# Attention and MoE on one core: DMA transposes replaced by PE transposes, weights cast by DMA, x in a ring

## The chip, the cores and the metric

The kernel runs on one core of one Trainium2 chip. The metric is the device time of one execution in microseconds (us); the median of several runs is quoted. "Span" is the time from the first to the last instruction in the profiled execution; it is about 2 us shorter than the time. The names of engines: PE is the matmul engine, ACT ScalarE, DVE VectorE, Pool GpSimd, SP the engine that here only issues DMAs.

## The reference, cut to what matters

Attention over 8 batches, 8 heads, 576 tokens, head size 64, with a causal window of 128 and an ALiBi bias; its output, as x of 4608 tokens by 512, goes through a two-layer network:

```python
scores = (1/8) * q @ k.T + slopes[h] * -(i - j)     # kept where 0 <= i - j < 128
x = softmax(scores) @ v                             # -> [8 * 576, 512]
h = x @ w_in                                        # [4608, 2048]    "moe1"
out = (h * cos(h)) @ w_out                          # [4608, 512]     "moe2"
```

Inputs and output are float32; the kernel computes in bf16 with float32 sums.

## The kernel before

Tokens go through moe1 and moe2 in nine chunks of 512; attention goes by batches of 576. After a start (loads, masks, attention of batch 0), seven stages alternate: moe1 of chunk c, 64 dense matmuls, then attention of batch c + 1, whose short matmuls are filled up with the 64 moe2 matmuls of chunk c. A tail finishes the last two chunks.

Attention needs q and k with the head dimension on the partitions, and moe1 needs x so. For batches 1 to 7 all three are transposed by the DMA engines, issued from SP.

```python
def dma_transposes(b):                     # q and k of batch b, two DMAs each
    for which in ("q", "k"):
        fns = [lambda e: e.dma_start_transpose(<blocks 0 to 3 of tr[which][b % 2]>, nat[which] ...),
               lambda e: e.dma_start_transpose(<block 4>, ...)]
        op("sp", fns, ...)
...
def x_dma(b, pr):                          # x of batch b, one pair of heads, 512 tokens
    ...
    fns.append(lambda e, o=o, i=i: e.dma_start_transpose(o, i))
    op("sp", fns, r=[("xnat", b % 2, pr, 0), ("xnat", b % 2, pr, 1)],
       w=[("xT", b, pr)] + (stages if t0 + 512 > XA else []), dma=f"x{pr}{b % 2}")
```

`op` records what an operation reads (`r`) and writes (`w`) and puts the waits in. Tokens beyond 2560 (`XA`) have their x in a buffer that is the weights' staging buffer under another name, so `w` names all its parts (`stages`). The loop (cut) runs over nine units of attention a batch, one of tails and eight of a pair of heads and half of the tokens. `scores` is the product of q and k (PE), `exps` the exponential (ACT), `mask` the multiplication by the mask (DVE), `pv` the product with v (PE), `norm` the division by the sum of a row (DVE); `take(n)` issues the next n fill matmuls, those of moe2:

```python
take(lead)                                 # lead = 8 moe2 matmuls
for j in range(2): scores(us[j]); exps(us[j])
for j in range(n):                         # n = 9
    take(per)                              # per = 4 moe2 matmuls, ahead of the scores
    mask(us[j])
    if j + 2 < n: scores(us[j + 2]); exps(us[j + 2])
    if j >= 1: norm(us[j - 1]); after_norm(us[j - 1])    # issues x_dma
    pv(us[j])
    if mid is not None and j == n // 2: mid()
...
def mid(c=c):                              # in the middle of attention of batch c + 1
    if c + 2 < B: dma_transposes(c + 2); load_v(c + 2)
    if c + 3 < B: load_nat("q", q, c + 3); load_nat("k", k, c + 3)
```

The weights come as float32 through a staging buffer by SP and are cast to bf16 by DVE.

The softmax here doesn't subtract the row's maximum and nothing guards it: scores larger than these inputs give would overflow.

## Time and profile before

446.1 us (445.0 to 448.9, 3 runs); span 444.3 us.

| part | us of the span | what shows |
|---|---|---|
| start | 0 to 48.6 | attention of batch 0 waits for q's copies, which stand behind weight casts on DVE, and then for v |
| seven stages | 48.6 to 385.5: 46.0, 47.3, 45.4, 57.1, 53.4, 45.2, 42.6 | PE waits for DMA before moe1 |
| tail | 385.5 to 444.3 | PE dense |

From the page of the kernel before: PE's busy tenths and the granted PE clock in 40 slices of 11 us, and the chain of work that ended last.

```profile
PE   0057798849794979697840997619885988899996
PEclk9999998969897898989895798958998898999999
...
PE 53%; DMA 19%; DVE 12%; SPq 6%; ACT 5%; issue 2%; POOL 2%; DVEq 0%; ACTq 0%; POOLq 0%
```

PE is often below nine tenths, and the clock falls with it. SPq, SP's issue queue, has 6% of the chain. The table of waits, PE's lines: what PE waited for, us in total, times, the longest.

```profile
PE ps L610 <- DMA wstage<-xnat: 35.4, 4, 16.7
PE ps L610 <- DMA xTa<-xnat: 16.9, 3, 6.4
PE ps L487 <- DVE xnat L512: 14.3, 7, 2.1
...
PE ps L487 <- DVE p L453: 8.6, 10, 1.1
```

L610 is moe1, L487 the product with v (PV). So PE waits 52.3 us for x's transposes ahead of moe1, and 22.9 us inside attention.

The table of stretches (window; its length; busy us of PE, weight loads, DVE, ACT, Pool with counts; PE clock; DMA share; GB/s) gives the start of moe1 of stage 1, that moe1, its attention, and a moe1 with a wait of only 1.3 us before it:

```profile
94.50:98.00 3.50, 3.48 (x9) 1.30 (x10) 0.69 (x1) 0.69 (x1) 3.05 (x4) 0.50 2.14 198
94.50:110.70 16.20, 16.13 (x64) 6.94 (x66) 9.72 (x15) 10.31 (x15) 3.05 (x4) 0.86 1.06 81
110.70:135.40 24.70, 20.74 (x189) 9.57 (x190) 13.83 (x33) 11.39 (x12) 4.74 (x6) 0.93 0.64 95
385.50:399.50 14.00, 13.91 (x64) 6.39 (x66) 9.70 (x15) 10.30 (x15) 0.00 (x0) 1.00 0.08 30
```

Behind the wait the clock is 0.50 for 3.5 us, and moe1 takes 16.2 us instead of 14.0.

### The profile page before, as it was taken

What the parts mean: (1) busy time and instruction counts of PE and PEld (TensorE: products, weight loads), DVE (VectorE), ACT (ScalarE), POOL (GpSimd) and SP (SyncE); (2) the same over time, 40 slices, a digit from 0 to 9 for tenths busy, and PEclk for the clock granted to TensorE, in tenths of its full rate; (3) what the DMA queues carried; (4) which work ended last, traced back from release to release, by engine and by line L of the source; (5) the groups of instructions that cost most, each with busy time, mean ns of one, the idle gap of its engine ahead of it and who ended that gap; (6) DMA issues with size and microseconds to landing.
All of it is one profiled execution on the core that took longest, in us unless ns stands there. A gap on an engine that the chain in (4) does not pass through costs nothing.

```text
span 444.3 us, 5753 instructions
## 1 busy us (share of the span) xinstructions
PE 329.3 (74%) x2231; PEld 152.1 (34%) x2268; DVE 228.9 (52%) x444; ACT 190.8 (43%) x245; POOL 97.8 (22%) x123
## 2 busy tenths in 40 slices
PE   0057798849794979697840997619885988899996
PEld 0044343314341434243320443304342433444442
DVE  2737795617560666266620456406572556474531
ACT  3044584317540664077410573206750673374320
POOL 8801047370037001710064000820000000000000
PEclk9999998969897898989895798958998898999999
DMA  9999599994199906990499004990064002300111
GB/s 221 266 270 130 194 156 133 173 190 27 31 137 188 60 26 116 189 86 26 81 145 130 36 1 95 163 157 0 8 122 127 0 2 65 84 0 25 43 51 72
DMA packets 166363, 44.76 MB, mean 101 GB/s; under 512 B 154560, under 2 KB 159680, under 8 KB 166336
## 3 DMA queue, kind: packets, MB, share of 16 engines
q0 software_dynamic: 104224, 14.16, 53.3%
q1 hardware_dynamic: 62112, 30.22, 27.8%
q8 instruction: 18, 0.29, 0.3%
q14 instruction: 9, 0.07, 0.0%
HBM read 36.70 MB, written 9.44 MB: 104 GB/s over the span
## 4 chain that ended last, share of the span: by engine, by line
PE 53%; DMA 19%; DVE 12%; SPq 6%; ACT 5%; issue 2%; POOL 2%; DVEq 0%; ACTq 0%; POOLq 0%
PE ps L610 29%; PE ps L632 17%; DMA wstage<-xnat 11%; DMA vp<-in_v_dram 5%; DMA xTa<-xnat 4%; DVE ob L637 2%; DVE p L453 2%; SPq L552 2%; PE ps L487 2%; DVE gT L618 2%; PE ps L415 2%; ACT L430 2%; SPq L258 2%; SPq L261 2%; DVE xnat L512 2%
## 5 line engine op out<-in xcount | busy, mean ns | idle before, releaser
L615 ACT ACTIVATE cos<-ps,halfpi 128x512 f32<-128x512 f32 x144 | 98.8, 687 | 144.4 <-PE ps L610 143.9
L618 DVE TENSOR_TENSOR gT<-ps,cos 128x512 bf16<-128x512 f32 x144 | 98.8, 690 | 108.6 <-ACT cos L615 108.6
L632 PE MATMUL ps<-w_outb,gT 128*128 128x512 bf16 x552 | 140.4, 391 | 1.9 <-issue 0.9
L610 PE MATMUL ps<-xTa,w_inb 128*128 128x512 bf16 x312 | 78.9, 415 | 35.4 <-DMA xTa<-xnat 16.9
L439 ACT ACTIVATE p<-ps 128x768 bf16<-128x768 f32 x64 | 58.0, 917 | 67.2 <-PE ps L415 62.9
L610 PE MATMUL ps<-wstage,w_inb 128*128 128x512 bf16 x251 | 63.2, 404 | 19.1 <-DMA wstage<-xnat 18.7
L632 PEld LDWEIGHTS ps<-w_outb,gT 128*128 128x128 bf16 x576 | 52.5, 100 | 54.7 <-issue 4.9
L240 POOL DMA_DIRECT2D qnat<-in_q_dram x35 | 29.8, 875 | 167.6 <-DMA qt<-qnat 167.6
L610 PEld LDWEIGHTS ps<-xTa,w_inb 128*128 128x128 bf16 x320 | 33.4, 106 | 80.6 <-issue 48.9
L637 DVE COPY ob<-ps 128x512 f32<-128x512 f32 x36 | 24.9, 691 | 56.6 <-PE ps L632 56.6
L610 PEld LDWEIGHTS ps<-wstage,w_inb 128*128 128x128 bf16 x256 | 26.1, 103 | 53.8 <-issue 27.3
L487 PE MATMUL ps<-vp,p 128*128 128x65 bf16 x256 | 25.3, 207 | 22.9 <-DVE xnat L512 14.3
L453 DVE TENSOR_TENSOR p<-p,emask 128x768 bf16<-128x768 bf16 x64 | 39.5, 616 | 0.4
L249 POOL DMA_DIRECT2D vp<-in_v_dram x40 | 34.0, 900 | 11.7 <-issue 11.7
L240 POOL DMA_DIRECT2D knat<-in_k_dram x35 | 30.1, 883 | 13.5 <-DMA kt<-knat 13.2
L487 PEld LDWEIGHTS ps<-vp,p 128*128 128x128 bf16 x256 | 18.3, 105 | 34.1 <-DVE xnat L512 15.9
L522 DVE TENSOR_TENSOR xnat<-ps,rec 128x256 bf16<-128x256 f32 x64 | 27.2, 424 | 2.2
L415 PE MATMUL ps<-qt,kt 64*128 64x128 bf16 (+1 forms) x320 | 26.7, 269 | 1.1 <-ACT ptail L430 0.8
L490 PE MATMUL ps<-vp,p 128*128 128x65 bf16 x192 | 22.6, 206 | 0.0
L415 PEld LDWEIGHTS ps<-qt,kt 64*128 64x128 bf16 x320 | 11.4, 100 | 27.0 <-issue 14.3
L367 PE MATMUL ps<-ident,gT 128*64 128x128 bf16 x72 | 4.5, 314 | 21.6 <-DVE qt L380 11.0
L521 DVE RECIPROCAL rec<-ps 128x4 f32<-128x4 f32 x64 | 11.4, 177 | 13.8 <-PE ps L490 12.8
(47 smaller groups left out, 127.0 us busy)
## 6 DMA issues: line engine op xcount, KB each, us to landing
out_dram<-ob SPq DMA_DIRECT2D x36, 256.0 KB, 2.3
wstage<-in_moe_w_in_dram SPq DMA_DIRECT2D x8, 512.0 KB, 12.5
vp<-in_v_dram POOLq DMA_DIRECT2D x32, 128.0 KB, 6.7
wstage<-in_moe_w_out_dram SPq DMA_DIRECT2D x8, 512.0 KB, 9.3
qnat<-in_q_dram POOLq DMA_DIRECT2D x28, 128.0 KB, 6.5
knat<-in_k_dram POOLq DMA_DIRECT2D x28, 128.0 KB, 6.1
gT<-in_q_dram POOLq DMA_DIRECT2D x2, 288.0 KB, 7.4
gT<-in_k_dram POOLq DMA_DIRECT2D x2, 288.0 KB, 10.6
```

The source lines that it names most:

```text
L240: fns.append(lambda e, t=t, rows=rows: e.dma_start(nat[which][0:rows, t, :, :], src[b, :, 128 * t:128 * t + rows, :].rearrange("h p d -> p ...
L249: fns.append(lambda e, t=t, rows=rows: e.dma_start(vp[b % 2][0:rows, t, :, 0:64], v[b, :, 128 * t:128 * t + rows, :].rearrange("h p d -> p ...
L415: ins = e.matmul(ps[:, banks[x], c0:c1], keys_ap(b, x, pr, kc), query_ap(b, x, pr, qb, nb), start=True, stop=True)
L439: op("act", lambda e: e.activation(P[i][:, :, lo:512], ps[:, 2 * slot:2 * slot + 2, lo:512], ACTF.Exp, scale=0.125), w=[("B", 2 * slot), ( ...
L453: op("dve", lambda e: e.tensor_tensor(P[i][:, :, lo:512], P[i][:, :, lo:512], EM[:, 2 * pr:2 * pr + 2, lo:512], ALU.mult), r=[("P", i), "E ...
L487: ins = e.matmul(o, P[i][:, x, d0:d0 + 128], V[:, kc, h, 0:65], start=True, stop=not two)
L522: op("dve", lambda e: e.tensor_tensor(o, U[:, :, :, 0:64], rv[:, :, :, None].broadcast_to([128, 2, 2, 64]), ALU.mult), r=[("rec", n % 2)], ...
L610: ins = e.matmul(ps[:, bank, :], w_in[:, kc, 128 * fc:128 * fc + 128], rhs, start=(kc == 0), stop=(kc == NPAIR - 1))
L615: op("act", lambda e: e.activation(cosb[ci][:, :], ps[:, bank, :], ACTF.Sin, bias=halfpi[:, 0:1]), r=["halfpi"], w=[("B", bank), ("cos", ci)])
L618: op("dve", lambda e: e.tensor_tensor(gT[gi][:, fc, :], ps[:, bank, :], cosb[ci][:, :], ALU.mult), r=[("cos", ci)], w=[("B", bank), ("g", ...
L632: op("pe", lambda e: e.matmul(ps[:, bank, :], gT[gi][:, fc, 128 * t:128 * t + 128], w_out[:, fc, :], start=(fc == 0), stop=(fc == NFC - 1) ...
L637: op("dve", lambda e: e.tensor_copy(ob[oi][:, :], ps[:, bank, :]), w=[("B", bank), ("ob", oi)])
```

## The change

Its intent: no DMA transposes at all. q and k come in long rows (2304 bytes each) and are transposed on PE, in moe1, for every batch; x is transposed on PE unit by unit and copied out by ACT into a ring of three chunks; the weights are cast on the way in by DMAs from Pool, so that staging buffer and DVE casts go; v of batch 0 comes ahead of the weights. The masks have the band in the exponent, so no DVE multiply. The fill is split, two moe2 matmuls ahead of the scores and three ahead of PV. The diff, cut to its core:

```diff
-        stage = sb("wstage", [128, NST, 1024], F32)
-        xTa = sb("xTa", [128, NPAIR, XA])
-        xTb = stage[...]...
+        XR = 3 * CH
+        xT = sb("xT", [128, NPAIR, XR])
...
+        def load_w_in(u):
+            op("pool", lambda e: e.dma_start(
+                w_in[:, :, 512 * u:512 * u + 512],
+                moe_w_in[:, 512 * u:512 * u + 512].rearrange("(k p) c -> p k c", p=128)),
+               w=[("wi", u)], dma=f"wi{u}")
...
+        def x_back(b, u, n, eng):
+            bank = ubanks(u, n)[0]
+            dst = ps[:, bank, :].bitcast(BF16)[:, 768:1024]
...                    two PE transposes of 128 x 128, then the copy on ACT
+            for j in range(n + 2):
+                take(part[0] if j < n else last)
+                if 2 <= j:
+                    x_back(b, us[j - 2], j - 2, "act")
+                if j + 2 < n:
+                    scores(b, us[j + 2], j + 2)
+                    exps(b, us[j + 2], j + 2)
+                if j < n:
+                    take(part[1])
+                    pv(b, us[j], j)
+                if j + 1 < n:
+                    mask(b, us[j + 1])
+                if j < n:
+                    norm(b, us[j], j)
...
+                steps = iter(qk_transposes([6, 7], ["dve", "act"]))
                 for fc in range(NFC):
                     moe1(c, fc)
-                    if c == 0 and fc % 2 == 1:
-                        cast_w(8 + fc // 2, "dve")
+                    if fc % 2 == 1:
+                        next(steps)()
...
-                attention(c + 1, moe2_steps(c), 8, 4, mid=mid)
+                attention(c + 1, moe2_steps(c), (8, (2, 3), 3))
```

## The prediction

> **What bounds the kernel now.** The matmul engine (PE) is busy 329 of 444 us, yet the chain of waits gives it only 53%, and DMA 19%. The time is a start (to 48.5 us), seven stages (to 385.5 us: moe1 of a chunk, then attention of the next batch filled with moe2) and a tail (58.8 us).
>
> - Start: attention of batch 0 waits for v until 32.0 us (timeline; 22.4 us of v's DMA in the chain), because the weights share the DMA engines.
> - Stages take 46, 47, 46, 57, 53, 45, 42 us. By the table of waits, PE before moe1 waits 16.9 us for x's DMA transposes into xTa and 35.4 us into the weight staging: 52 us. Behind each gap the clock comes back at 0.50 (94.5 to 98 us), and moe1 takes 16.2 us against 13.9 where there was no gap (385.5 to 399.5): 2.3 us six times. The Trainium skill, "TensorE: Matmul & The Clock Gate", part 1, says that an idle window halves the PE clock; the trace agrees.
> - Tail: PE dense at clock 0.99 to 1.00; untouched.
>
> **The change, costed.** Removed: 52 us of waits, about 14 us of cold restarts, 16 weight casts on DVE (12 us). Added per stage:
> - q/k transposes: batch 0 did 36 in 2.13 us, so 72 take 4.3 us of PE; eight evacuations, four on DVE (0.82 us), four on ACT (0.74 us). In moe1 DVE and ACT then need 14.3 and 15.2 us of 18: hidden; PE's 4.3 us are not.
> - x transposes: 20, about 1.2 us of PE, and nine ACT copies of about 0.4 us, hidden unless a bank waits for them.
> - Attention with moe2 has about 19.5 us of warm PE work and took 20 to 25; five fill matmuls a unit in place of four should close the 2.1 and 1.0 us gaps before PV. I estimate 22.5 us with x.
>
> Stage: 18.2 + 22.5 = about 41 us; seven are 287, against 337.
>
> Start: DMAs by GpSimd alone moved 155 GB/s written, 310 read (30 to 41 us). q, k and v are 3.5 MB and land near 15 us; attention of batch 0, bound by latency at about 1.5 us a unit, ends near 31; w_in is there by 28, q and k of batch 1 by 35, w_out by 48, v by 51 us (15.5 MB): just in time. Moe1 starts near 32 us, 16 earlier.
>
> Sum: 32 + 287 + 59 = 378 us of span, 380 with the 2 us between span and time. With a little for stalls: **383 us, eight times in ten 366 to 405.** Faster by over 2%: 0.95; within 2%: 0.03; slower: 0.02.
>
> **What would show each step.** No DMA wait of PE before moe1 after the first stage; moe1 matmuls at about 216 ns from the first; moe1 with transposes 18 us; stages of 40 to 42 us; first moe1 at 30 to 35 us; about 16 ACT table loads; mean clock over 0.95; PE busy over 85%.
>
> **What would make it wrong.**
> 1. The clock. The same page, part 4, says that transposes don't count as PE activity. 1.0 us of them after each 1.7 us of matmuls may drop the clock: moe1 phases of 21 us or more, 20 us in all. Batch 0's transposes ran at clock 1.00, but with no matmuls around them.
> 2. Weights cast by DMA slower than 300 GB/s read, or w_out and v of batch 1 late: stage 0 stalls by 5 to 10 us.
> 3. ACT in strict order: an x copy queued behind an exp holds a bank, and PV waits, about 0.5 us a unit: 30 us in all.
> 4. The start's latency chain per unit no shorter than before: 5 us.

## More of the kernel before

In the start, DVE's timeline and PE's waits show two things behind each other:

```profile
15.10 0.85 DVE L298 CAST w_inb<-wstage 128x1024 bf16<-128x1024 f32 x1 [2.58 <-DMA wstage<-in_moe_w_in_dram]
21.43 0.82 DVE L380 COPY qt<-ps 128x640 bf16<-128x640 bf16 x1
PE ps L473 <- DMA vp<-in_v_dram: 2.7, 1, 2.7
```

Four weight casts, each waiting for its weights, and then the masks stand on DVE ahead of q's first copy, at 21.4 us although q had landed at 10.1; v landed last, at 31.9, but cost PE only 2.7 us more.

One view I did not look at closely before predicting is SP's timeline (start, us, engine line, operation), here of stage 0:

```profile
75.23 1.19 SPq L552 DMA_TRANSPOSE xTa<-xnat  x1
76.47 3.14 SPq L258 DMA_TRANSPOSE qt<-qnat  x1
79.65 1.26 SPq L261 DMA_TRANSPOSE qt<-qnat  x1
80.95 2.14 SPq L258 DMA_TRANSPOSE kt<-knat  x1
83.13 1.53 SPq L261 DMA_TRANSPOSE kt<-knat  x1
84.71 0.58 SPq L640 DMA_DIRECT2D out_dram<-ob  x1
85.33 4.77 SPq L552 DMA_TRANSPOSE xTa<-xnat  x3
```

One pair of heads of x is issued at 75.2; then SP spends 8.2 us on issuing q and k of the next batch, which nobody needs before the next attention, a whole moe1 later; the other three pairs of x, which moe1 needs at once, go out from 85.3 on. Their norms had ended at 80.4, 82.6 and 84.7 us; they landed at 92.2, 93.0 and 94.3.

## The result, and the profile after

366.0 us (365.6 to 367.2, 4 runs) against 446.3 us (4 runs). The outputs are right. A ratio here is the mean time of one kernel's runs over that of the other's of the same rounds, so not quite the ratio of the medians; it is 0.82, with a 95% interval of 0.816 to 0.824. The direction was right and well within what was called likely, but the time is at the very edge of the range (366 to 405), 17 us below the 383 that was named. The lines of the page that answer to those of before:

```profile
PE   0688999999999999999999999999999999999996
PEclk9955999999999999999999999999999999999999
...
PE 79%; ACT 10%; DVE 6%; DMA 2%; issue 1%; POOL 1%; ACTq 0%; DVEq 0%; POOLq 0%
```

From slice 5 on PE is busy nine tenths or more at full clock; DMA has 2% of the chain instead of 19%. PE's lines in the table of waits (L290: q/k transposes, L342: scores, L414: PV, L505: moe1), the longest and those for moe1 and PV:

```profile
PE ps L290 <- DMA qrows<-in_q_dram: 8.8, 1, 8.8
PE ps L342 <- ACT ptail L357: 4.4, 7, 0.6
...
PE ps L414 <- DVE rec L443: 0.8, 5, 0.2
PE ps L414 <- ACT xT L487: 0.7, 2, 0.5
...
PE ps L505 <- ACT xT L487: 0.2, 1, 0.2
```

The 52.3 us ahead of moe1 are 0.2 us; the 22.9 us ahead of PV are under 3 (1.8 on L414). The stretches: moe1 of stage 1 with its 72 transposes, its attention, and the moe1 of the tail without transposes.

```profile
71.93:89.84 17.91, 17.91 (x139) 7.94 (x137) 13.78 (x20) 13.43 (x21) 1.32 (x3) 1.00 0.20 37
89.84:111.07 21.23, 20.44 (x212) 10.36 (x211) 13.33 (x32) 14.20 (x26) 5.37 (x7) 1.00 0.80 104
306.73:320.55 13.82, 13.82 (x66) 6.27 (x64) 10.41 (x16) 10.97 (x16) 0.00 (x0) 1.00 0.05 20
```

| part | before | predicted | after |
|---|---|---|---|
| first moe1 starts at | 48.6 | 32 | 30.6 |
| seven stages together | 337.0 | 287 | 276.0 (41.1, then six times 39.1) |
| tail | 58.8 | 59 | 58.7 |

### The profile page after: what moved, and what is told of

Its sections match the earlier page's. It is cut to its first block, busy times and chain, and to the rows that moved or that the text cites. A ratio compares the mean times of both kernels' runs of the same rounds, so it can differ in the third digit from the quotient of the medians.

```text
span 365.3 us, 7057 instructions
## 1 busy us (share of the span) xinstructions
PE 341.4 (93%) x2912; PEld 164.6 (45%) x2912; DVE 233.1 (64%) x446; ACT 234.5 (64%) x352; POOL 61.3 (17%) x89
## 4 chain that ended last, share of the span: by engine, by line
PE 79%; ACT 10%; DVE 6%; DMA 2%; issue 1%; POOL 1%; ACTq 0%; DVEq 0%; POOLq 0%
PE ps L505 33%; PE ps L528 30%; PE ps L290 5%; PE ps L342 5%; ACT cos L511 3%; ACT L357 2%; DMA krows<-in_k_dram 2%; PE ps L414 2%; ACT ptail L357 2%; PE ps L473 2%; PE ps L417 1%; ACT kt L303 1%; DVE kt L306 1%; DVE ob L533 1%; DVE gT L514 1%; DVE p L380 1%
## 5 line engine op out<-in xcount | busy, mean ns | idle before, releaser
L528 PE MATMUL ps<-w_outb,gT 128*128 128x512 bf16 x576 | 151.4, 380 | 0.0
L505 PE MATMUL ps<-xT,w_inb 128*128 128x512 bf16 x576 | 138.5, 384 | 0.2 <-ACT xT L487 0.2
L505 PEld LDWEIGHTS ps<-xT,w_inb 128*128 128x128 bf16 x576 | 52.6, 98 | 62.2 <-issue 2.4
L366 ACT ACTIVATE p<-ps 128x768 bf16<-128x768 f32 (+1 forms) x64 | 57.6, 915 | 6.2 <-PE ps L342 6.2
L487 ACT ACTIVATE xT<-ps 128x256 bf16<-128x256 bf16 (+3 forms) x80 | 28.9, 363 | 48.5 <-PE ps L473 42.8
L380 DVE TENSOR_TENSOR p<-p,emask 128x768 bf16<-128x768 bf16 (+1 forms) x64 | 39.5, 616 | 1.1 <-ACT p L366 0.9
L210 POOL DMA_DIRECT2D qrows<-in_q_dram x16 | 10.1, 640 | 172.4 <-PE ps L290 171.6
L342 PE MATMUL ps<-qt,kt 64*128 64x128 bf16 (+1 forms) x320 | 24.6, 248 | 5.4 <-ACT ptail L357 4.4
L414 PEld LDWEIGHTS ps<-vp,p 128*128 128x128 bf16 x256 | 18.3, 100 | 17.4 <-ACT xT L487 8.4
L414 PE MATMUL ps<-vp,p 128*128 128x65 bf16 x256 | 23.1, 198 | 2.2 <-DVE rec L443 0.8
L290 PE MATMUL ps<-ident,qrows 128*64 128x128 bf16 x288 | 15.0, 239 | 8.8 <-DMA qrows<-in_q_dram 8.8
L473 PE MATMUL ps<-ident,xnat 128*128 128x128 bf16 x128 | 18.6, 230 | 1.4 <-DVE xtail L435 1.2
L290 PEld LDWEIGHTS ps<-ident,qrows 128*64 128x64 bf16 x288 | 10.0, 119 | 21.0 <-issue 12.3
L473 PEld LDWEIGHTS ps<-ident,xnat 128*128 128x128 bf16 x128 | 12.3, 101 | 14.9 <-DVE xtail L435 1.4
L342 PEld LDWEIGHTS ps<-qt,kt 64*128 64x128 bf16 x320 | 11.4, 96 | 16.4 <-ACT ptail L357 7.8
```

The costliest lines, as they stand in the source:

```text
L290: ins = e.transpose(dst[64 * x:64 * x + 64, 128 * (j - j0):128 * (j - j0) + 128], qB[which][:, 2 * pl + x, 64 * j:64 * j + 64], ident[:, :])
L342: ins = e.matmul(ps[:, banks[x], c0:c1], keys_ap(x, pr, kc), query_ap(x, pr, qb, 128 * nb), start=True, stop=True)
L366: op("act", lambda e: e.activation(P[i][:, :, lo:512], ps[:, 2 * slot:2 * slot + 2, lo:512], ACTF.Exp, scale=0.125), w=[("B", 2 * slot), ( ...
L380: op("dve", lambda e: e.tensor_tensor(P[i][:, :, lo:512], P[i][:, :, lo:512], EM[:, 2 * pr:2 * pr + 2, lo:512], ALU.mult), r=[("P", i), (" ...
L414: ins = e.matmul(o, P[i][:, x, d0:d0 + 128], V[:, kc, h, 0:65], start=True, stop=not two)
L473: ins = e.transpose(dst[:, 128 * r:128 * r + 128], xnat[n % NX][:, 128 * r:128 * r + 128], ident[:, :])
```

## The experiments

Names that begin with b are the kernel before with parts of the change or other edits, those with a the kernel after with parts undone. Each time is a median of four runs, with the ratio to the kernel before on the same chip. Stage lengths below are read from the starts of moe1 in each timeline.

### b_qkmove: q and k issued after x

Was it the transposing by DMA that made PE wait, or what stood ahead of x in SP's queue?

```diff
                 def mid(c=c):
                     if c + 2 < B:
-                        dma_transposes(c + 2)
                         load_v(c + 2)
-                    if c + 3 < B:
-                        load_nat("q", q, c + 3)
-                        load_nat("k", k, c + 3)
                 attention(c + 1, moe2_steps(c), 8, 4, mid=mid)
+                if c + 2 < B:
+                    dma_transposes(c + 2)
+                if c + 3 < B:
+                    load_nat("q", q, c + 3)
+                    load_nat("k", k, c + 3)
```

> The kernel before, with the DMA transposes of q and k (and the loads behind them) issued after attention instead of in its middle. Theory A (the x transposes waited in SP's issue queue behind 8 us of q/k transposes): the waits into xTa (16.9 us) nearly vanish, with a cold restart of 2.3 us each; the waits into the staging buffer shrink by half at most, since there a second cause is at work; 415 to 430 us. Theory B (a DMA transpose of x takes 5 us or more by itself): the waits before moe1 stay near 52 us and the time near 446.

Measured: 389.2 us, ratio 0.873 (0.869 to 0.876). A few lines in another place give 57 of the change's 80 us. In the table of waits no line for DMA into xTa is left, and the other one is:

```profile
PE ps L610 <- DMA wstage<-xnat: 7.8, 4, 3.9
```

Moving them was enough, and I had even underestimated it: the staging waits fell from 35.4 to 7.8 us, not by half at most. SP's part in it: the Trainium skill, "DMA: Bandwidth & Descriptors", section "Anatomy of one DMA" (written for DMAs from GpSimd), says that the wait for a semaphore happens on the issuing sequencer and not in the DMA engines. So whatever stands ahead on SP, an issue or a wait, holds back all that follows. The timeline of before agrees: the last x of stage 0 was normed at 84.7 us and issued at 88.8; in this run, 86.16 and 86.18.

But the edit did a second thing that the theory doesn't name. It also took the transfers of q and k, by SP and by Pool, off the time in which x is in flight. The transposes of x into xTa, median us from issue to landing, before and in this run:

```profile
xTa<-xnat SPq DMA_TRANSPOSE x19, 5.4
xTa<-xnat SPq DMA_TRANSPOSE x19, 2.4
```

For that last x it is 5.4 against 2.4 us. So of the 7.2 us by which it landed sooner behind its norm, 4.1 came from SP's queue and 3.0 from a quicker transfer. No run parts the two; issuing q and k later cures both.

### b_qkmove_nostage: without the false write

```diff
-               w=[("xT", b, pr)] + (stages if t0 + 512 > XA else []), dma=f"x{pr}{b % 2}")
+               w=[("xT", b, pr)], dma=f"x{pr}{b % 2}")
```

(and the same for the tail of x). The casts of the weights, which last read that buffer, lie on DVE ahead of the norms that x waits for, so the order holds without it; the check for races agrees.

> As b_qkmove, and the x transposes into the aliased staging buffer no longer name that buffer as a write, which had made each wait for the one before it to land. Theory A with this second cause: nearly all 52 us of waits and most of the 14 us of cold restarts go, 385 to 400 us. Theory B: still 430 or more.

Measured: 378.9 us, ratio 0.850 (0.847 to 0.853), below the range that was expected. In the chain of before, the three x transposes ahead of the last moe1 stand one behind the other, from issue to landing:

```profile
376.45 2.40 DMA wstage<-xnat
...
378.86 4.02 DMA wstage<-xnat
...
382.90 2.39 DMA wstage<-xnat
```

With the false write gone they overlap, and the wait that is left in this run is one of 1.8 us:

```profile
PE ps L610 <- DMA wstage<-xnat: 1.8, 1, 1.8
```

So DMA transposes of q, k and x can all be kept, with 1.8 us of such waits left to PE. Two edits to what is written in which order are worth 67 us here; the change as a whole is worth 80.

### b_xpe: x alone on PE

The kernel before with `x_back` as in the kernel after (two transposes a unit, ACT copies them out, one unit after its norm); q and k stay with the DMA engines, in the middle of attention.

> The kernel before, with x alone transposed on PE for all batches, two transposes a unit, copied out by ACT. My prediction's ledger: minus 52 us of waits and 14 us of cold restarts, plus about 9 us of PE: about 390 us. Rival (an x copy in ACT's order holds PV's bank): PV waits of about 0.5 us a unit, 405 to 420 us.

Measured: 397.5 us, ratio 0.893 (0.889 to 0.897), between the two expectations. All waits for x are gone, but PV waits for the copies:

```profile
PE ps L487 <- ACT wstage L616: 7.0, 21, 0.5
PE ps L487 <- ACT xTa L616: 6.5, 20, 0.5
```

Those are 13.5 us, the third danger that the prediction named, here with the old placing of the fill. In the kernel after the same line has 0.7 us.

### a_xdma: x alone back to DMA

```diff
-            op("pe", f, r=rk + ["ident"], w=[("B", bank)])     # and the copies on ACT
+            fns.append(lambda e: e.dma_start_transpose(
+                xT[:, pr, r0:r0 + 256].rearrange("p (t r) -> p t r", r=128), src[:, :]))
+            ...                     # where the ring wraps: four pieces of 64 tokens
+            op("sp", fns, r=[("xnat", n % NX)], w=xkeys(pr, t0, 256), dma=f"x{n % NX}")
```

> The kernel after, with x alone back to DMA transposes (256 tokens each), q and k still on PE. Theory A: SP's queue holds nothing else, the last x transposes land about 3.5 us after their norm against 2.4 us of fill left, and PE saves 1.2 us a stage: 362 to 375 us. Theory B (each x transpose costs 5 us or more at the end of a stage, and the restart is cold): 395 us or more.

Measured: 416.2 us, ratio 0.933 (0.929 to 0.937). By the numbers that is Theory B, but the stages say otherwise: 43.2, 56.9, 43.7, 39.5, 53.9, 41.8 and 39.1 us, and the first moe1 at 37.9 us. Two stages are as short as in the kernel after. The two long ones are those whose batch wraps around the ring, where my variant cuts the transposes into 64 tokens. SP's timeline in one of them:

```profile
109.06 1.24 SPq L465 DMA_TRANSPOSE xT<-xnat  x1
110.34 5.62 SPq L471 DMA_TRANSPOSE xT<-xnat  x4
...
117.89 5.04 SPq L471 DMA_TRANSPOSE xT<-xnat  x4
```

An issue takes about 1.2 us, whether it moves 64 tokens or 256 (medians of the run 1.23 and 1.20). The two wrapped stages are 32.6 us of the 50 us by which this run is slower than the kernel after, the start 7.3 us, and the other five stages together 9.8 us. So the run prices SP's queue once more, by my variant's own doing; it is no verdict on DMA transposes, for which `b_qkmove_nostage` stands.

### a_front4 and a_fill4: the fill

What closed the gaps ahead of PV? Both runs give the kernel after four fill matmuls a unit, as before.

```diff
-                attention(c + 1, moe2_steps(c), (8, (2, 3), 3))
+                attention(c + 1, moe2_steps(c), (8, (4, 0), 3))     # a_front4: all ahead of the scores
+                attention(c + 1, moe2_steps(c), (8, (2, 2), 3))     # a_fill4: two ahead of PV
```

> The kernel after, with the fill as before: four moe2 matmuls a unit, all ahead of the scores. My prediction took it that the fill closes the 2.1 and 1.0 us gaps before PV and allowed 1.3 to 1.8 us a stage for what stays open. Theory C (the fill's count or place closes them): PV waits of 2 to 3 us a stage come back, 380 to 388 us. Rival (the new order of norm and mask closed them, not the fill): 364 to 370 us.

> The kernel after, four fill matmuls a unit, but split as after: two ahead of the scores and two between scores and PV. If the place matters and not the count: at most 0.5 us a stage, 366 to 370 us. If the count matters: 375 us or more.

Measured: `a_front4` 385.3 us (ratio 0.863, 0.860 to 0.865), `a_fill4` 370.2 us (0.829, 0.827 to 0.832). The place is worth about 15 us, the fifth matmul about 4 us. PE's longest wait in attention of `a_front4`, and what the same line is in `a_fill4`:

```profile
PE ps L414 <- ACT xT L487: 12.2, 33, 0.7
```

```profile
PE ps L414 <- ACT xT L487: 1.0, 3, 0.5
```

By the code, PV of unit j needs the bank (a part of PSUM, the memory into which PE writes) that the copy of unit j - 2 leaves, and that copy stands in ACT's order behind an exponential. With two matmuls between scores and PV, 0.43 us, 3 of the 33 waits are left. These are not the waits of before, which were for DVE (14.3 and 8.6 us): in `a_front4`, with all fill in front, DVE has about 1 us of PV's waits (on L414), so the rewritten loop had closed those, as the rival says, and the place keeps new ones for ACT's copies away. In `b_all23` below, with the old loop, the split fill takes the old waits from 22.8 (`b_qkmove_nostage`) to 2.4 us.

### b_wcast: the weights alone

The kernel before with `load_w_in` and `load_w_out` as in the kernel after, on Pool behind v of batch 0, and no DVE casts.

> The kernel before, with the weights alone cast by DMA from GpSimd behind v of batch 0, in after's order. Theory D (the weights on the shared DMA engines delayed v): v lands near 16 us, the first moe1 starts at 33 to 37 us instead of 48.5, the rest is unchanged: 430 to 435 us. Rival (the time is given back in stage 0, as q and k of batch 1, w_out and v of batch 1 come later): 440 us or more.

Measured: 438.0 us, ratio 0.982 (0.976 to 0.987); less than 2%, so by that measure not clear. The first moe1 starts at 38.0 us instead of 48.6, and the stages are about 1 us longer in total than before. The weights did delay v as supposed, which lands at 15.1 us instead of 31.9, but neither range was met, and v is the smaller part: q's first copy on DVE starts at 13.4 us instead of 21.4, as no cast stands ahead of it, which is 8.0 of the 10.5 us; PE's wait for v was 2.7. The run removed both together; v alone, by the trace of before, could have given 2.7 at most. The timeline of DVE in the next run, which has the same start, shows what is now first in line, the masks and then the first copy of q, which had landed at 6.6 us there:

```profile
7.54 4.62 DVE L324 TENSOR_TENSOR emask<-gT 128x2048 bf16<-128x2048 f32 x2 [4.60 <-ACT gT L317]
12.19 1.64 DVE L330 COPY emtail<-emask 128x256 bf16<-128x256 bf16 x4
13.39 0.82 DVE L361 COPY qt<-ps 128x640 bf16<-128x640 bf16 x1
```

### b_all23: the four cheap edits together

`b_qkmove_nostage` and `b_wcast`, and the fill split as in the kernel after:

```diff
-                take(per)
+                take(2)
                 mask(b, us[j])
...
+                take(3)
                 pv(b, us[j], j)
```

> The kernel before with DMA transposes kept for q, k and x, but q and k issued after attention, no false write of the staging buffer, weights cast by DMA, and the fill split 2 and 3 as after. Theory A+C+D: each stage loses the PV waits and pays no PE transposes: stages of about 35 us, first moe1 near 35 us: 335 to 348 us, below the kernel after. Rival: with 11 fill matmuls (2.4 us) left behind the last norm instead of 20, x lands late, 2 us or more a stage with cold restarts: 355 to 375 us.

Measured: 349.8 us, ratio 0.784 (0.781 to 0.787): 16 us below the kernel after, with all DMA transposes of batches 1 to 7 kept. It is 2 us above the expected range: the first moe1 starts at 38.0 us instead of near 35, and x is a little late, as the rival had it, but only by 7.4 us in all:

```profile
PE ps L591 <- DMA wstage<-xnat: 4.4, 3, 2.4
...
PE ps L591 <- DMA xTa<-xnat: 3.0, 3, 1.0
PE ps L468 <- DVE p L434: 2.4, 9, 0.8
```

A usual stage is 35.3 us (38.6 in `b_qkmove_nostage`): of the 3.1 us of PV waits a stage, 0.2 are left.

### b_best23 and b_best22x: the best version tried

`b_best23` adds the masks of the kernel after; `b_best22x` moves fill from the loop to behind it: `take(2)` ahead of PV instead of 3, but 6 at the second unit, whose PV waits for the long norm of the tails.

> As b_all23, with the masks built as in the kernel after (the band is in the exponent, so no DVE multiply of 4.6 us ahead of the first q evacuation). Theory: the q evacuation starts at 7 to 8 us instead of 13.4, the first moe1 at 33 to 35 us instead of 38.0, all else equal: 344 to 347 us. Rival (k's DMA lands too late for it to matter): 349 us.

> As b_best23, with four fill matmuls a unit and eight at the second unit, so that 16 instead of 11 are left behind the last norm for x's DMA transposes. Theory: the 7.4 us of waits for x go, and PV waits of less than 1 us a stage come: 338 to 344 us. Rival (the attention loop itself is as long as its ACT and DVE work, and what is moved behind it is lost ahead of it): the same as b_best23 or 2 us more.

Measured: `b_best23` 349.3 us (ratio 0.783, 0.779 to 0.787), `b_best22x` 344.7 us (0.774, 0.769 to 0.780). The first is a miss: moe1 starts at 35.9 us, as the copy of the tails' mask still stands ahead of q's evacuation, until 11.2 us, and the 2 us won are lost in stage 0 (38.9 against 37.0 us); 1.1 us of that is a wait for k of batch 1, and by the traces most of the rest is clock: the moe1 of stage 0 starts at half clock in both, and as it starts earlier here, 13 matmul starts are 427 ns apart instead of 9, about 0.7 us. The second is 0.7 us above its range, and its theory held in part: the waits for x fell from 7.4 to 5.3 us and did not go; PV's fell too (L459 in the table of waits, from 2.4 to 1.3), and usual stages are 34.3 to 34.8 us. It is the fastest correct version here, 21 us below the kernel after.

### a_noqkt and a_qkt2: the price of transposes on PE

```diff
-                    if fc % 2 == 1:
-                        next(steps)()                          # a_noqkt: q and k of batch 0 for all
```

```diff
-                                for j in range(j0, j1):
+                                for j in [*range(j0, j1)] * 2:     # a_qkt2: each transpose twice
```

> The kernel after without the q/k transposes of batches 1 to 7 (q and k of batch 0 are used for all; the result is wrong on purpose). If the 72 transposes a stage cost what PE shows for them (4.0 us), seven stages lose 28 us: 336 to 340 us. If they were partly hidden: 345 us or more.

> The kernel after with every q/k transpose done twice (result right). If transposes cost PE time alone and the clock holds: plus 28 to 32 us, 394 to 400 us, clock 1.00 in moe1. If transposes do not count as activity and half of moe1 being transposes drops the clock: 410 us or more, clock under 0.9 in moe1.

Measured: `a_noqkt` 338.3 us (0.758, 0.754 to 0.762), 27.7 us less than the kernel after, as expected: each stage is 35.1 us instead of 39.1, so the PE transposes of q and k are paid in full. This run computes attention with the wrong q and k and still passes the comparison. Inputs are a tenth of a normal draw, so the scores are so small that the bias decides. The comparison therefore can't vouch for q and k; for the runs with moved q/k transposes it is the check for races that does.

`a_qkt2`: 379.4 us (0.851, 0.847 to 0.856), 13.4 us more; neither expectation was met. The clock held: moe1 of stage 1 in that run, with 144 transposes,

```profile
72.70:92.40 19.70, 19.22 (x206) 9.87 (x209) 13.86 (x20) 13.43 (x20) 1.25 (x2) 1.00 0.19 35
```

has clock 1.00. But the second 72 cost only 1.8 us a stage (40.9 against 39.1), 25 ns each, where the first 72 cost 4.0 us. So the price has a part by group, not by transpose. PE's timeline in the kernel after and in this run shows a group of 10 and one of 20:

```profile
82.41 0.47 PE L290 MATMUL ps<-ident,qrows 128*64 128x128 bf16 x10
82.81 1.90 PE L505 MATMUL ps<-xT,w_inb 128*128 128x512 bf16 x8
```

```profile
74.55 0.75 PE L290 MATMUL ps<-ident,qrows 128*64 128x128 bf16 x20
75.23 1.90 PE L505 MATMUL ps<-xT,w_inb 128*128 128x512 bf16 x8
```

From the start of a group to the next matmul it is 0.40 us for 10 and 0.68 us for 20, so 28 ns for each further one and about 0.12 us for the group. The starts of the single instructions in the kernel after show the rest. Moe1's matmuls start 216 ns apart, but the first transpose of a group 309 ns after the matmul ahead of it; the pairs then follow at 56 ns, with 24 more for the second; and moe1 goes on 151 ns after the last one. That makes about 0.09 us on the way in, 0.02 at the second pair and 0.11 on the way out, or 1.8 us for eight groups; with 36 pairs at 56 ns it comes to 3.8 of the 4.0 us.

## Why the prediction was right or wrong

The prediction had the right direction and the right large terms, and it failed by its size.

1. **The step that failed: "I estimate 22.5 us with x"** for attention with moe2. It took 21.2 us. I had added to 19.5 us of warm PE work and 1.2 us of x transposes some 1.8 us for waits that would stay; PE waits 0.8 us there (0.6 for the tails' exponentials, 0.2 ahead of PV, in stage 1), beside 20.4 us of work. With the rounding of 18.2 + 22.5 up to 41, and moe1 at 17.9 us, a stage was put at 41 and six of seven were 39.1: 11.0 us over seven stages. `a_front4` and `a_fill4` show why there was so little left to wait for: I credited the fifth matmul, which is worth 4 us in all, and took no account of the place between scores and PV, which is worth 15.
2. The rest of the 17 us: the start was 1.4 us shorter than named, the tail 0.3 us, 3 us were added by hand "for stalls" that did not come, and the profiled run whose span is used here is 1.2 us slower than the median. All went the same way. The low end lay 14 us under my own sum of 380 us of time and should have covered that error; I guarded against four dangers and none of the opposite kind.
3. **The 52 us of waits and the cold restarts: right.** They went (0.2 us left), and moe1 starts at full clock in stages 1 to 6. The Trainium skill's "TensorE: Matmul & The Clock Gate", part 1, says that an idle window halves the clock; both traces agree for moe1 (0.50 behind gaps of 4.3 us and more, 1.00 behind one of 1.3 and in the kernel after). Inside attention gaps of 2.0 us were enough (four times in `b_qkmove_nostage`). One fall is left without a cause: in the kernel after the clock is 0.50 from 18.0 to 35.1 us, in attention of batch 0, though in the 3.4 us before PE had no gap over 1.1 us and was busy for 2.0. What I did not see was the cause of the waits. I took them as the price of transposing x by DMA, though SP's timeline showed x standing behind 8.2 us of q and k. `b_qkmove` and `b_qkmove_nostage` show that the waits came of an order, which held x back in SP's queue and put q's and k's transfers beside it, and of a false write. The change removed them by removing the queue's contents.
4. **The PE price of q and k: right** in size (4.3 us named, 4.0 us measured by `a_noqkt` and by the stretches), but by luck. `a_qkt2` shows 25 ns for a further transpose, not 59. The 59 came from batch 0, which I took to run at clock 1.00; there was no record yet, and its pairs start 107 ns apart, against 56 in moe1 at a recorded 1.00. So I priced them at half clock, and the 1.8 us of getting into and out of eight groups, which I had left out, happen to be nearly as much.
5. **The start: right in its end** (32 named, 30.6 measured), not in what had held it: v, which I named, was 2.7 us of it, and the weight casts ahead of q's copy on DVE 8.0. `b_wcast` shows 10.5 us of the 18 from these two, `b_best23` 2.2 from the masks; the other 5.3 are not taken apart.
6. **Dangers.** The clock did not fall with transposes in moe1, not even with twice as many; transposes alone even raised it (the last section). The weights' DMAs were in time: the stage they feed, 41.1 us, is longer than the others by 2 us, and moe1 there starts cold (clock 0.88 over its first 19 us; 4.5 us at 0.50 are worth 2.2). The danger of ACT's order is real, 12 to 13.5 us in `b_xpe` and `a_front4`, and the kernel after avoids it by where its fill stands.

Where the 80 us came from, as far as the experiments take it apart: 67 us is what the two edits of order win from the kernel before (446 to 379). The split fill, the early v and the rest of the start win 29 us more (379 to 350, with DMA transposes kept). The kernel after reaches the like by other means: without its q and k transposes (`a_noqkt`) it takes 338 us, 12 less than `b_all23`, 8 of them in the start. But it pays about 28 us for q and k on PE, and comes to 366. Its trade was a good one against the kernel before and a poor one against what the kernel before could be.

## What to carry to other kernels

Before replacing a slow-looking transfer, read the timeline of the queue that issues it: what is needed at once must not stand behind what is needed later, and a buffer used under two names should not make writers wait for each other. Put fill work between the producer's last instruction and the consumer that needs a buffer freed, rather than ahead of both. Before taking a clock or a price from a stretch, check that a clock record covers it; the distance between like matmuls tells. When every term of a forecast has been given an allowance for waits that might stay, lower the low end by their sum.

## What the Trainium skill lacked or had wrong

- "DMA: Bandwidth & Descriptors", section "Issuing engines are not separate DMA queues", calls the time on the sequencer to initiate a DMA "usually small relative to the DMA itself". For DMA transposes issued from SP here it was not: 1.2 to 3.1 us an issue in stage 0, about 1.2 us even for 64 tokens, against 2.3 to 5.4 us from issue to landing (medians), and up to 8.7 us in the start of `b_wcast`, beside the weights' DMAs. Moving such issues (8.2 us in stage 0), with the loads behind them, out of x's way gave 57 us of 446.
- "TensorE: Matmul & The Clock Gate", part 4, says that full clock doesn't engage for transposes, which don't count as PE activity in the same way. Here it did. In `a_qkt2` PE had done nothing but transposes since the run began when the first clock record, 1.00, came at 13.7 us, and within one pair the distance between pairs went from 107 to 56 ns while the transposes went on; in the kernel after, too, the record at 14.6 us stands behind transposes alone. And in moe1 with 72 and with 144 transposes among 64 matmuls the clock was 1.00.
- The same part gives about 275 ns for a transpose in a kernel. That is a duration, and here one of q or k lasts 219 to 243 ns at a recorded clock of 1.00 and 314 at half clock. It gives no price in a dense stream, where transposes overlap: 4.0 us for 72 in eight groups, and 25 ns for each further one (transposes of 64 columns, in pairs to the two halves of the array).
- No page was found that says where fill matmuls should stand between the uses of a shared PSUM bank; here the place was worth 15 us of 385.
